# The down projection of the last two token blocks by two levels of seven products, in an attention and SwiGLU kernel

## The chip, the cores and the metric

One core of a Trainium2 chip runs the kernel; the other cores are idle. The metric is the time of one execution on the device in microseconds. The profile is that of one execution, taken by the hardware profiler; its times count from the first instruction of the program.

## The reference

Everything is float32. The attention has no softmax: for each of 8 batches and 8 heads `kv = k^T v` (64 x 64) and `out = q kv`, then an RMS norm over the 64 features of the head with a gain. The heads side by side give 4608 token rows of 512 features. The feed-forward part is

```python
g = x @ w_gate                          # 4608 x 512 by 512 x 1536
silu = g * (1.0 / (1.0 + np.exp(-g)))
val = x @ w_val                         # 512 x 1536
return silu * val @ w_out               # 1536 x 512
```

## The kernel before

The tokens are cut into 9 blocks of 512 (`NB` = 9). Each block has an attention part (`Att`), an up phase (gate and value products, then `silu(g) * val`, whose result `h` stands with the 1536 features on partitions) and a down phase (`h` times `w_out`). Blocks 0, 1, 2 run alone; from block 3 on (`PAIRED`) two blocks go through the up phase together (`Pair.up`), and then down one after the other (`Ffn.down` for `pair.a`, then for `pair.b`). The last pair is blocks 7 and 8, and no attention work lies beside it.

The matrix products use the Winograd form of Strassen's scheme: both operands are cut in 2 x 2 quadrants and seven products of sums take the place of eight. Product numbers 1 to 7 name them; `CHAIN` says in which of three PSUM accumulators (`a`, `b`, `c`) each product lands and whether it starts it. Products 1, 6, 7, 4 follow each other in one bank of `b`, and 5, 3 in one of `c`. Between two products of one bank the sum so far is copied or added out to SBUF, so the next product has to wait for that eviction. The pools hold three banks of `b`, two of `c`, one of `a` and two of `m` (scratch).

In a pair's up phase two levels of the scheme are nested: 7 outer times 7 inner products. It runs in 6 units (`j`), each with 4 groups of outer products (`Inner.GROUPS` = (1, 5), (6, 2), (7), (4, 3)), each group with 7 inner products. A group of two outers issues two 128x256 matmuls per product, a group of one issues one. Group 0 evicts mostly by ScalarE copies, all other evictions are VectorE additions. The last two products of a group (3 and 4) are issued inside the sequence of the next group. `made1`, `made2` and `made3` hold what follows: GpSimd adds partial results, ScalarE applies Silu, GpSimd multiplies the two halves into `h` (for the last unit VectorE does), and `h_sums` forms the side sums that the down phase of block a needs, again on GpSimd. The weights of the up phase, 49 leaf sums per unit, were written to DRAM once and are streamed through nine `t` tiles (`Stream`): a load goes out when the tile nine loads back is free.

The down phase before is one level: 7 products per block, each 6 steps (`NP`) times 2 output halves of 128x256, so 84 matmuls per block, with `h` as the stationary operand and `w_out` or a sum of its quadrants as the moving one. GpSimd forms these sums (`turn_t`) and the side sums of block b (`second_sums`). With no further block the last pair uses the branches marked `lone`, and block 8 also those marked `final`: product 3 goes into its own banks of `m`, is split in two halves, and each half is added and stored on its own, so that the end is short.

The order of instructions on an engine comes from a list scheduler that works in the program's trace order and takes what it thinks is ready. `in_order(engine)` pins an engine to trace order; before, it holds for TensorE in the down phases of pairs. `tc.issue_after(ins)` queues the instructions traced inside it behind `ins`, on the engine of `ins` alone; it makes nothing wait for `ins` to finish. In a queue each engine works in order: an instruction that waits holds all behind it.

Lines that matter: 661 the matmuls of `Quad`, 816 those of `Inner`, 1032 those of `third`; 130, 131 and 132 the helpers `add`, `sub` and `mul` (most vector work has one of these lines, whatever it is for); 494 and 510 transposes of the attention part on TensorE and VectorE; 1122 the output stores.

Of the kernel before, what the change touches and what calls it, by code (L numbers as in the profile page):

```python
# [18 lines left out]
def kernel(  # L19
# [620 lines left out]
    class Quad:  # L640


        def __init__(self, steps):
            self.steps = steps
            self.ps, self.room = {}, None

            self.apart = {}

# [3 lines left out]
        def multiply(self, p):  # L652
            name, first = CHAIN[p]
            if first:
                tiles = [PSUMS[name].tile([P, 2, HB], F32, name=name) for _ in range(1 + (name in self.apart))]
                self.ps[name], self.apart[name] = tiles[0], tiles[-1]
            banks = self.ps[name], self.apart[name]
            for e, i in self.order(p):
                lhsT, rhs = self.operands(p, e, i)

                self.ffn.multiplied = nc.tensor.matmul(  # L661
                    banks[e][:, e], lhsT=lhsT, rhs=rhs, start=first and i == 0 and (e == 0 or banks[0] is not banks[1]),
                    stop=i == self.steps - 1, skip_group_check=True,
                )
# [92 lines left out]
    class Inner:  # L757
# [94 lines left out]
        def made3(self, p, e, q):  # L852
# [7 lines left out]
            mul(engine, h[:, :, :, 0:HB], halves(c11), halves(c12))  # L860
            with tc.issue_after(self.ffn.fifth.ins):
                nc.scalar.activation(out=c21, in_=c21, func=ACT.Silu)
            mul(engine, h[:, :, :, HB:BLK], halves(c21), halves(c22))
            self.ffn.ended = self.ffn.a.h_sums(self.j, 1, engine)

# [13 lines left out]
    class Stream:  # L879
# [15 lines left out]
        def pump(self):  # L895

            while self.next and not self.held[-9]:
                n, j, c = key = self.next.pop(0)
                tile_ = t_tile(key)
                os, ps = JOINT[c]  # L900
# [6 lines left out]

        def use(self, n, j, o, p):
            c, i = self.joint[o, p]
            key = n, j, c  # L910
# [74 lines left out]
    class Down(Quad):  # L985
        def __init__(self, ffn):
# [3 lines left out]
            self.final = ffn.n == NB - 1  # L990
            self.lone = False
            self.opens = None
            self.keeps = False
            if self.final:
                self.apart["c"] = None
# [16 lines left out]
        def multiply(self, p, es=(0, 1)):  # L1012
            if p == 3 and self.lone:
                self.third(es)
                return
# [7 lines left out]
        def third(self, es):  # L1023


            if es[0] == 0:
                tiles = [m_psum.tile([P, 2, HB], F32, name="m") for _ in range(1 + self.final)]
                self.thirds = tiles[0], tiles[-1]
            for e in es:
                for i in range(self.steps):  # L1030
                    lhsT, rhs = self.operands(3, e, i)
                    self.ffn.multiplied = nc.tensor.matmul(  # L1032
                        self.thirds[e][:, e], lhsT=lhsT, rhs=rhs, start=i == 0 and (e == 0 or self.final),
                        stop=i == self.steps - 1, skip_group_check=True,
                    )
            if not self.final:
                add(nc.vector, self.o1[:, :, HD:DM], self.thirds[0], self.u2)
                self.ffn.store(self.o1, 0)
                return
            for e in es:  # L1040
                add(nc.vector, self.o1[:, e, HD:DM], self.thirds[e][:, e], self.u2[:, e])
                self.ffn.store(self.o1[:, e : e + 1, HD:DM], e, slice(HD, DM))

        def after6(self):
            super().after6()
            if self.lone:
                self.add_c(self.u2, self.u2)

        def order(self, p):
            order = [(e, i) for e in range(2) for i in range(self.steps)]  # L1050
            return order if p == 3 and self.final else sorted(order, key=lambda ei: ei[1])
# [17 lines left out]
        def rows(self):  # L1069
            o = ring()  # L1070
            self.o1, self.o2 = o[:, 0:2], o[:, 2:4]

        def after2(self):
            if self.lone:
                self.rows()
            add(nc.vector, self.o1[:, :, 0:HD], self.ps["a"], self.s)
            if self.final:
# [398 lines left out]
```

## Time and profile before

| | us |
|---|---|
| median of 3 runs | 1013.04 (1010.67 to 1013.1) |
| the profiled execution | 1012.7 |
| its span, first to last instruction | 1010.9 |
| TensorE busy | 993.7 |
| VectorE busy | 673.7 |
| GpSimd busy | 369.6 |
| last up phase, blocks 7 and 8 | 807.6 to 934.9 |
| last down phases, blocks 7 and 8, TensorE | 934.9 to 1007.5 |
| from there to the end of the span | 3.4 |

The profile has one row for each group of like instructions: start, how long they took together, engine, line, operation, output <- inputs, shape, count. A number in brackets at the end is idle time of the engine before it and who ended it. `PE` is TensorE, `DVE` VectorE, `ACT` ScalarE, `POOL` GpSimd, `SPq` SyncE's DMA queue. A float32 matmul leaves two records, so a count of 24 means 12 matmuls. In a table of windows the columns are the window's length, then busy time and number of instructions of PE, PEld (weight loads), DVE, ACT and POOL, the granted TensorE clock, the busy share of the DMA engines and GB/s.

### The profile page before, as it was taken

What the parts mean: (1) busy time and instruction counts of PE and PEld (TensorE: products, weight loads), DVE (VectorE), ACT (ScalarE), POOL (GpSimd) and SP (SyncE); (2) the same over time, 40 slices, a digit from 0 to 9 for tenths busy, and PEclk for the clock granted to TensorE, in tenths of its full rate; (3) what the DMA queues carried; (4) which work ended last, traced back from release to release, by engine and by line L of the source; (5) the groups of instructions that cost most, each with busy time, mean ns of one, the idle gap of its engine ahead of it and who ended that gap; (6) DMA issues with size and microseconds to landing.
All of it is one profiled execution on the core that took longest, in us unless ns stands there. A gap on an engine that the chain in (4) does not pass through costs nothing.

```text
span 1010.9 us, 17078 instructions
## 1 busy us (share of the span) xinstructions
PE 993.7 (98%) x6506; PEld 831.6 (82%) x6506; DVE 673.7 (67%) x1121; ACT 232.2 (23%) x367; POOL 369.6 (37%) x290
## 2 busy tenths in 40 slices
PE   5999999999999999999999999999999999999998
PEld 4544688888888888888888888888888888888887
DVE  2999797589868477656676746666668566666311
ACT  2665111221122311212211121121112121121000
POOL 0000263255544240445456004455660026546600
PEclk9999999999999999999999999999999999999999
DMA  8688653483866855767742464667221654553011
GB/s 220 198 266 260 120 93 136 97 288 97 210 136 122 214 114 158 189 179 182 170 130 42 111 164 135 182 164 191 77 42 43 146 164 144 150 145 101 1 42 42
DMA packets 254290, 143.23 MB, mean 142 GB/s; under 512 B 149504, under 2 KB 236544, under 8 KB 254208
## 3 DMA queue, kind: packets, MB, share of 16 engines
q1 hardware_dynamic: 223488, 138.20, 50.8%
q10 hardware_dynamic: 30656, 3.94, 2.5%
q8 instruction: 52, 0.85, 0.4%
q14 instruction: 30, 0.25, 0.1%
q0 software_dynamic: 64, 0.00, 0.0%
HBM read 104.99 MB, written 28.70 MB: 132 GB/s over the span
## 4 chain that ended last, share of the span: by engine, by line
PE 75%; DMA 1%; POOL 0%; SPq 0%; issue 0%; DVE 0%; POOLq 0%
PE b L816 22%; PE b L661 20%; PE c L816 11%; PE c L661 9%; PE a L816 5%; PE a L661 5%; PE m L431 1%; PE m L1032 1%; PE m L370 1%; DMA ld<-in_v_dram 1%; POOL t L131 0%; SPq L312 0%; PE b L370 0%; PE b L431 0%; PE a L431 0%
## 5 line engine op out<-in xcount | busy, mean ns | idle before, releaser
L816 PE MATMUL b<-arena,t 128*128 128x256 f32 x1008 | 244.5, 381 | 0.0
L816 PEld LDWEIGHTS b<-arena,t 128*128 128x128 f32 x1008 | 190.1, 190 | 29.6 <-DVE r L130 2.4
L130 POOL TENSOR_TENSOR r<-r 128x256 f32<-128x256 f32 (+1 forms) x90 | 94.7, 1054 | 246.1 <-DVE r L130 154.9
L130 DVE TENSOR_TENSOR r<-b,r 128x512 f32<-128x512 f32 (+1 forms) x234 | 138.9, 606 | 60.1 <-PE b L816 54.8
L130 DVE TENSOR_TENSOR r<-c,r 128x512 f32<-128x512 f32 (+1 forms) x170 | 104.5, 623 | 81.9 <-PE c L816 40.1
L132 POOL TENSOR_TENSOR arena<-r 128x1024 f32<-128x1024 f32 (+1 forms) x54 | 102.1, 1904 | 112.3 <-DVE r L130 67.9
L131 POOL TENSOR_TENSOR t<-wo 128x512 f32<-128x512 f32 x54 | 76.9, 1445 | 167.8 <-DVE wo L130 105.9
L130 DVE TENSOR_TENSOR r<-a,r 128x512 f32<-128x512 f32 x93 | 59.2, 636 | 108.3 <-PE a L661 70.7
L816 PE MATMUL c<-arena,t 128*128 128x256 f32 x504 | 122.5, 379 | 0.0
L131 DVE TENSOR_TENSOR arena<-arena 128x512 f32<-128x512 f32 (+3 forms) x96 | 104.3, 1101 | 20.0 <-PE b L661 17.7
L816 PEld LDWEIGHTS c<-arena,t 128*128 128x128 f32 x504 | 95.6, 190 | 13.5 <-issue 0.3
L661 PE MATMUL b<-wo,arena 128*128 128x256 f32 x432 | 98.1, 382 | 0.2
L661 PE MATMUL b<-t,arena 128*128 128x256 f32 x432 | 96.2, 379 | 0.0
L661 PEld LDWEIGHTS b<-wo,arena 128*128 128x128 f32 x432 | 81.2, 190 | 12.5 <-DVE arena L132 0.9
L661 PEld LDWEIGHTS b<-t,arena 128*128 128x128 f32 x432 | 82.1, 190 | 11.2
L830 ACT COPY r<-b 128x512 f32<-128x512 f32 x54 | 31.7, 586 | 189.9 <-PE b L816 189.9
L131 POOL TENSOR_TENSOR t<-arena 128x512 f32<-128x512 f32 x36 | 51.1, 1432 | 56.2 <-PE c L661 21.9
L816 PE MATMUL a<-arena,t 128*128 128x256 f32 x252 | 66.1, 379 | 0.0
L816 PEld LDWEIGHTS a<-arena,t 128*128 128x128 f32 x252 | 47.9, 190 | 6.5
L661 PE MATMUL c<-t,s 128*128 128x256 f32 x216 | 48.1, 379 | 0.0
L661 PE MATMUL a<-wo,arena 128*128 128x256 f32 x216 | 48.1, 379 | 0.0
L661 PEld LDWEIGHTS a<-wo,arena 128*128 128x128 f32 x216 | 41.0, 190 | 5.6
(115 smaller groups left out, 1242.9 us busy)
## 6 DMA issues: line engine op xcount, KB each, us to landing
t<-w SPq DMA_DIRECT2D x180, 256.0 KB, 3.1
out_dram<-r SPq DMA_DIRECT2D x17, 512.0 KB, 2.9
ld<-in_k_dram SPq DMA_DIRECT2D x26, 288.0 KB, 4.6
ld<-in_v_dram SPq DMA_DIRECT2D x26, 288.0 KB, 6.1
t<-w SPq DMA_DIRECT2D x54, 128.0 KB, 2.3
ld<-in_moe_w_gate_dram SPq DMA_DIRECT2D x12, 512.0 KB, 4.6
ld<-in_moe_w_val_dram SPq DMA_DIRECT2D x12, 512.0 KB, 4.7
ld<-in_moe_w_out_dram SPq DMA_DIRECT2D x12, 512.0 KB, 4.8
```

The source lines that it names most:

```text
L130: add = lambda e, o, a, b: e.tensor_tensor(out=o, in0=a, in1=b, op=OP.add)
L131: sub = lambda e, o, a, b: e.tensor_tensor(out=o, in0=a, in1=b, op=OP.subtract)
L132: mul = lambda e, o, a, b: e.tensor_tensor(out=o, in0=a, in1=b, op=OP.mult)
L370: self.positions = nc.tensor.matmul(self.kv_ps[r][u * D : (u + 1) * D, g, :], lhsT=k[:, u, c, :], rhs=v[:, u, c, :], start=(c == 0), stop= ...
L431: self.multiplied = nc.tensor.matmul(self.ps[i][u][p : p + D, t, j, :], lhsT=self.qt[rows, tile_t, head, p : p + D], rhs=kvs[b % 3][rows, ...
L661: self.ffn.multiplied = nc.tensor.matmul(banks[e][:, e], lhsT=lhsT, rhs=rhs, start=first and i == 0 and (e == 0 or banks[0] is not banks[1 ...
L816: self.ffn.multiplied = nc.tensor.matmul(ps[:, i], lhsT=stream.use(self.ffn.n, self.j, o, p), rhs=self.operand(o, p), start=first and i == ...
L830: copied = nc.scalar.copy(out=dst, in_=ps)
L1032: self.ffn.multiplied = nc.tensor.matmul(self.thirds[e][:, e], lhsT=lhsT, rhs=rhs, start=i == 0 and (e == 0 or self.final), stop=i == self ...
```

## The change

For the last pair a new class `Deep` takes over the down phase of both blocks at once. It cuts `w_out` and `h` twice: 7 outer times 7 inner products, each of 3 steps of 128x128 weights against 256 columns (128 tokens of each block). Now the weight is the stationary operand and `h` the moving one, so the output comes out transposed, features on partitions. `Last` is the group class for it; its order of products and sums is written out by hand in `Deep.down`, inside `in_order` for TensorE and VectorE.

The sums of weight quadrants that this needs are formed on VectorE during the last up phase: `prepare` lists 6 turns of `w_out` in place, 12 sums that are kept, and 9 leaf groups (three sums and a DMA write to DRAM each); `tick`, called after each product of that phase, takes a step from the list at every second call, inside `tc.issue_after` of the product just traced. `made` replaces the last part of `made3`: the second multiplication, then the side sums of `h` for both blocks at once, and after every second unit the two sums of `turn` (the inner level's sums on `h`), put on `due` for 16 calls later. The 21 leaf weights come back through `Stream` in the `t` tiles. The sums on `h` of the inner level (`sum_x`) and of the outer level (`outer`) are made on VectorE inside the down phase.

At the end two of the four output corners are transposed on VectorE in 32x32 blocks and stored in 16 DMAs each, in runs of 32 floats (`send`; one corner through ScalarE's queue, one through SyncE's). The other two are transposed on TensorE, copied out by ScalarE, the last by VectorE, and stored in 8 DMAs (`turn_back`).

The branches `lone`, `final`, `third`, `apart` and `rows` go from `Quad`, `Down` and `Ffn`; blocks before the last pair never took them.

```diff
@@ class Inner, made3
             mul(engine, h[:, :, :, 0:HB], halves(c11), halves(c12))
+            if self.ffn.deep:
+                self.ffn.deep.made(self.j, engine, c21, halves(c21), halves(c22), h)
+                return
             with tc.issue_after(self.ffn.fifth.ins):
                 nc.scalar.activation(out=c21, in_=c21, func=ACT.Silu)
             mul(engine, h[:, :, :, HB:BLK], halves(c21), halves(c22))
             self.ffn.ended = self.ffn.a.h_sums(self.j, 1, engine)
+
+    class Last(Inner):
+        GROUPS = ((1, 2), (6, 5), (7,), (4, 3))
...
+        def multiply(self, p, cs=(0, 1, 2)):
...
+            for c in cs:
+                for i, o in enumerate(self.outers):
+                    self.ffn.multiplied = nc.tensor.matmul(
+                        ps[:, i], lhsT=self.deep.weight(o, p, c), rhs=self.deep.operand(o, p, c),
+                        start=first and c == 0 and i == 0, stop=c == 2, skip_group_check=True,
+                    )
...
+    class Deep:
+        LEAVES = (5, 7, 4)
...
+        def prepare(self, temp):
...
+            for i, o in enumerate(self.LEAVES):
+                b = self.quadrant({5: 3, 7: 1, 4: 2}[o])
+                for c in range(3):
+                    rows = slice(2 * c, 2 * c + 2)
+                    raw = temp[:, 0:4].rearrange("p (k n) d -> p k (n d)", k=2)
+                    self.later += [
+                        lambda b=b, rows=rows, raw=raw: sub(nc.vector, raw, b[:, rows], self.quadrant(6)[:, rows]),
+                        lambda: sub(nc.vector, temp[:, 4], temp[:, 0], temp[:, 1]),
+                        lambda: sub(
+                            nc.vector, temp[:, 5:7], temp[:, 2:4], temp[:, 1:2].to_broadcast([P, 2, P])
+                        ),
+                        lambda i=i, c=c: nc.sync.dma_start(out=self.dram[:, i, c], in_=temp[:, 0:7]),
+                        None, None,
+                    ]
+
+        def tick(self):
+            self.count += 1
+            if self.count % 2:
+                return
+            steps = self.later
+            if self.due and self.due[0][0] <= self.count:
+                steps = [self.due.pop(0)[1]]
+            step = steps.pop(0) if steps else None
+            if step:
+                with tc.issue_after(self.pair.multiplied.ins):
+                    step()
+
+        def made(self, j, engine, c21, g, v, h):
+            def second():
+                mul(engine, h[:, :, :, HB:BLK], g, v)
+                a11, a21, a22 = h[:, :, 0, 0:HB], h[:, :, 0, HB:BLK], h[:, :, 1, HB:BLK]
+                add(engine, a21, a21, a22)
+                sub(engine, a21, a21, a11)
+
+            with tc.issue_after(self.pair.fifth.ins):
+                nc.scalar.activation(out=c21, in_=c21, func=ACT.Silu)
+            if j == NP - 1:
+                self.second = second
+                return
+            second()
+            if j % 2:
+                self.due += [(self.count + 16, step) for step in self.turn(j // 2, (0, 1))]
...
+            return [lambda: add(nc.vector, a21, a21, a22), lambda: sub(nc.vector, a21, a21, a11)]
...
+        def send(self, room, half, cols, queue):
...
+                        queue.dma_start(
+                            out=dst.rearrange("(c i) j -> i c j", i=32), in_=t[32 * r : 32 * (r + 1), f, e]
+                        )
...
+        def down(self):
+            g = [Last(self, i) for i in range(4)]
...
+            m(0, 7)
+            self.outer(5, ((0, 0), (0, 1)))
+            m(0, 3)
+            m(1, 1)
...
+            m(2, 4)
+            nc.vector.transpose(out=room[:, 0], in_=c11)
+            self.send(room[:, 0], 0, 0, nc.scalar)
+            m(3, 6)
+            add(nc.vector, c22, u3, c22)
+            m(3, 5)
+            nc.vector.transpose(out=room[:, 1], in_=c22)
+            self.send(room[:, 1], 1, 1, nc.sync)
+            m(3, 2)
+            m(3, 7)
+            self.rows = ring().rearrange("p (e q) (o f d) -> p e q o f d", e=2, o=2, f=2)
+            m(3, 3)
+            self.turn_back(0, 0)
+            self.turn_back(1, 1)
+            m(3, 4)
+            self.turn_back(1, 0)
+            self.turn_back(0, 1, True)
@@ class Pair
-            a.down_ = Down(a)
-            a.down_.keeps = True
-            a.down_.turn_t(5)
+            if not deep:
+                a.down_ = Down(a)
+                a.down_.keeps = True
+                a.down_.turn_t(5)
@@ the loop over pairs
+        if pair.deep:
+            stream.leaves(pair.deep)
+            pair.up(fill)
+            with in_order(nc.tensor.engine, nc.vector.engine):
+                pair.deep.down()
+            continue
         pair.up(fill)
```

## The prediction

> **What bounds the kernel now.** I read the page's busy shares and its chain, then the windows over the last 200 us, then the timelines of one unit of the last up phase, and last a place where VectorE and GpSimd both work on SBUF.
>
> ```profile
> PE 993.7 (98%) x6506; PEld 831.6 (82%) x6506; DVE 673.7 (67%) x1121; ACT 232.2 (23%) x367; POOL 369.6 (37%) x290
> 811.00:935.00 124.00, 124.00 (x575) 108.87 (x574) 84.27 (x143) 24.00 (x33) 65.79 (x53) 1.00 0.47 139
> 935.00:1008.00 73.00, 72.54 (x337) 63.52 (x335) 16.77 (x20) 5.75 (x9) 16.29 (x12) 1.00 0.08 28
> ...
> 934.85 5.34 PE L661 MATMUL b<-wo,arena 128*128 128x256 f32 x24
> 1004.78 2.75 PE L1032 MATMUL m<-wo,arena 128*128 128x256 f32 x12
> 1007.58 0.42 DVE L130 TENSOR_TENSOR r<-m,r 128x256 f32<-128x256 f32 x1 [7.35 <-PE m L1032]
> ...
> 898.61 0.69 DVE L130 TENSOR_TENSOR r<-c,r 128x512 f32<-128x512 f32 x1
> 899.47 0.69 DVE L130 TENSOR_TENSOR r<-c,r 128x512 f32<-128x512 f32 x1 [0.17 <-PE c L816]
> 900.33 0.69 DVE L130 TENSOR_TENSOR r<-b,r 128x512 f32<-128x512 f32 x1 [0.17 <-PE b L816]
> 901.86 1.46 PE L816 MATMUL b<-arena,t 128*128 128x256 f32 x6
> 896.04 4.68 POOL L132 TENSOR_TENSOR arena<-r 128x1024 f32<-128x1024 f32 x2 [3.79 <-DVE r L130]
> 900.80 0.73 POOL L130 TENSOR_TENSOR s<-arena 128x256 f32<-128x256 f32 x1
> 901.60 0.73 POOL L131 TENSOR_TENSOR arena<-s,arena 128x256 f32<-128x256 f32 x1
> ...
> 138.61 3.16 DVE L131 TENSOR_TENSOR arena<-arena 128x512 f32<-128x512 f32 x2
> 138.25 9.40 POOL L131 TENSOR_TENSOR t<-arena 128x512 f32<-128x512 f32 x6 [1.33 <-DVE arena L130]
> ```
>
> TensorE is the bound and has no gap in the last up phase (124.00 of 124) or in the last down phase (72.54 of 73), so a product left out is worth its whole time, and a product that starts late costs its whole delay. A down product is 24 records from 934.85 to the next at 940.03, 0.216 us each; one 128x256 matmul is two records, 0.432 us. In the up phase VectorE is 68% busy and empties PSUM just behind TensorE, a 0.69 us eviction in each 0.86 us product, so its queue has little slack. The third block is unit j = 4 of that phase: evictions of (group 1, product 5), (group 0, product 3) and (group 1, product 6); the last must be out before group 1's product 7 reuses the bank at 901.86. Beside them GpSimd multiplies (896.04) and forms the side sums of the unit before (900.80, 901.60).
>
> **What the Trainium skill says.** "GPSIMD Engine Reference", section 1 (Specifications), says that GpSimd's SBUF interfaces are shared with VectorE, with contention where a VectorE instruction has two SBUF inputs. The trace agrees strongly: from 138.61 on a 128x512 sum with both inputs in SBUF takes 1.58 us beside GpSimd, against 0.68 alone (800.31); each waits out the GpSimd instruction in hand. PSUM evictions have one SBUF input and stay at 0.69 beside GpSimd. "DMA: Bandwidth & Descriptors", Specifications, says that runs below 512 B make the DMA engine read, modify and write; no row of before stores such runs to HBM, so the trace is silent on that.
>
> **Down phase: what goes and what comes.** Before, two blocks x 7 products x 12 matmuls = 168; 72.5 us. After, 7 x 7 x 3 = 147 matmuls of the same form: 147 x 0.432 = 63.5, so 9.1 us go. Sixteen transposes come; the eight of the first attention block took 1.06 us less a 0.16 us tail, 0.113 each: +1.8. Between the last product and the last four transposes stands one 0.69 us eviction, of which 0.45 lies under the four transposes before it: +0.4. TensorE's down phase: 65.7, that is -6.8.
>
> VectorE gets 72 instructions there: 33 of 768 elements, 19 of 512, 13 of 256, 7 of 1024. By the pitch that rows of before show (0.60 for 512, 1.67 for 1536, 1.09 ns an element and 0.05), 53 us in 66. I laid them in their queue's order beside the products. Sums for product 5 of the first group end 5 us after the start and are wanted at 7.8; the nearest comes at the second group's product 1, whose sum ends about 14.7 and is wanted at 16.0. GpSimd is idle by then, so nothing is held. No stall: 0, and if every sum were a third slower, +3. The 21 leaf loads (192 KB, 2.8 us in before) run nine tiles ahead of TensorE on a DMA at 8%: nothing.
>
> The end: two corners leave by VectorE transposes and 16 stores each of 128 B runs (32 KB), one set from ScalarE's queue, one from SyncE's. The nearest rows are loads of 32 KB in such runs (2.3 us) and SBUF copies of 64 KB (3.5 us); I take 2.5. Four at a time per queue, SyncE's set starts 55 us into the phase and is issued at about 64; eight stores of 0.5 us follow, the last at 68.2, landed at 70.8. From TensorE's end that is 4.9 us, where before had 3.35 (1007.53 to 1010.88): +1.5. Down phase in all: -6.8 + 1.5 = **-5.3**. With stores of 5 us it would be +8.5 later.
>
> GpSimd loses the nine t<-wo sums and the second block's sums, which nothing waits for in time; free of charge. The dropped special cases for the last block only ran here.
>
> **Up phase: what is added.** 49 side sums on VectorE: 15 of 512 elements, 12 of 384, 9 each of 256 and 128, 4 of 1024; 23.9 us at the pitch above, in 39.7 idle us. Their amount fits; their places matter. The source hangs them behind a TensorE product, but that wrapper orders only instructions of the named instruction's own engine, and these are VectorE's: in the built program's order they stand where the scheduler found VectorE free. The first four sums on wo stand even before the phase's first eviction; there the inner sums end about 1 us later and meet about 1.7 us of slack: 0.
>
> (a) The turn of h rows. For units 0 and 1 its two 1024-element sums stand in unit 2, just before and behind the eviction (group 1, product 6); for units 2 and 3 in unit 4, before and behind (group 0, product 3). They wait for GpSimd's sums of the unit just finished. These now cover both blocks, 512 elements, 1.27 us each (the t<-wo row) instead of 0.73: done at 900.80 + 2.54 = 903.35 on the ruler above. Unit 2: sum 903.45 to 904.6, eviction to 905.2, wanted at 901.86: 3.3 us. Unit 4: sum to 904.6, eviction of product 3 to 905.2, second sum to 906.4, eviction of product 6 to 907.1: 5.2 late, less about 1.5 us of group 2 products that the new order puts ahead: 3.7. Together 7.0. From below 0 cannot be reached, as VectorE's queue is in order (2.5 each if GpSimd is a little quicker); above, 5.2 each.
>
> (b) The other sums hold VectorE when GpSimd has the interface. The 512-element sum of a leaf often follows (group 1, product 1), about 898.5, when the second 2.35 us multiplication has just begun: up to 2.2 us; the small ones after it wait out a 1.27 us sum. In unit 3: 900.75 + four rows of 0.6, 0.6, 0.3 and 0.69 plus 0.2 held gives 903.1 against 901.86, about 1.3 to 1.5. In unit 1 two such places, 0.6 and 0.7; in unit 3 another 0.5 before group 2's product 7; 0.1 elsewhere. Sum 3.5, bounds 0 and 5; other places find GpSimd idle. Each later product moves by these: nothing downstream wins them back.
>
> Sum: 7.0 + 3.5 - 5.3 = **+5.2** against the profiled execution of 1012.7 (1.8 around its span): 1017.9, rounded to 1018.0. The median shown is 1013.04, 0.3 above that execution, well inside this.
>
> **Rivals.** *B: the shared interface costs nothing in the new place*, only the in-order wait (a): 7.0 - 5.3 = +1.7, 1014.4. For it: only some of the leaf sums fall on a multiplication. Against: the rows from 138 on.
>
> *C, faster: the sums find their gaps.* If GpSimd's chain ends before VectorE gets to the turn, or TensorE's order gives other work to fill, the up phase loses 0 to 2 and the down phase's gain stands: 1007.5 to 1009.5, taken 1008. For it: 39.7 idle us for 23.9 of sums. Against: the eviction's deadline is 1.5 us, GpSimd's chain 7.3 us.
>
> *D, slower still: 128 B stores to HBM.* At 5 us each the queues drain at 1.25 us a store, ScalarE's copies of the turned tiles wait behind its 16, then SyncE's eight come last: 8.5 us more, 1026.5. It decides from about 3 us a store. For it: the skill's sentence. Against: 128 B reads land in 2.3.
>
> *E: leaf writes hold VectorE.* Its scratch tile is rewritten only when the write has landed (2.6 us for the nearest w<-r rows, some 3 us of room): up to +1 each in three places, near 1021.
>
> **How the numbers follow.** Forecast A 0.50 (own range 1015 to 1022), B 0.17, C 0.15, D 0.12, E 0.06. Likeliest: 1018.0. The range 1008 to 1026 leaves out half of C and half of D and less than that of the rest. A change below 0.3% (3 us) is what a measurement of this kernel can't tell from none; slower by more: most of A, D, E and a third of B, 0.67; within: most of B, a little of A and C, 0.17; faster: 0.16.
>
> **What would show it.** Right: TensorE gaps of some 3 us each in units 2 and 4 of the last up phase, released by a VectorE eviction behind a 1024-element sum that waits for GpSimd; shorter ones in units 1 and 3; the down phase about 66 us on TensorE with no gap but the 0.4 before the last transposes; 4 to 5 us from there to the end. Wrong: an up phase of 127 us as before (C); 128x512 sums at 0.68 beside GpSimd's multiplications (B); landing of the small stores above 3 us and ScalarE's turned copies late (D).

## The result, and the profile after

The changed kernel takes **1024.12 us** (median of 4 runs, 1023.04 to 1024.53), the kernel before 1012.34 beside it: ratio **1.0117, 95% interval 1.0099 to 1.0134**. It is slower, by 11.8 us; the forecast was 1018.0. The profiled execution has a span of 1022.3 us (before 1010.9).

In the kernel after, line 813 has the matmuls of `Inner` (816 before), 889 those of the new down phase, 1073 its transposes on TensorE, 1064 and 1083 the stores, 962 the leaf writes. First the busy shares on the page of after, then its windows over the last up phase and the last down phase:

```profile
PE 992.8 (97%) x6480; PEld 828.0 (81%) x6480; DVE 736.6 (72%) x1223; ACT 232.9 (23%) x370; POOL 357.6 (35%) x275
...
811.00:951.66 140.66, 130.46 (x575) 111.93 (x574) 106.73 (x188) 24.25 (x33) 70.11 (x50) 0.95 0.54 165
951.66:1018.00 66.34, 65.64 (x311) 57.34 (x309) 54.55 (x72) 6.55 (x12) 0.00 (x0) 1.00 0.27 64
```

The up phase is where the time is lost. TensorE runs the same 575 records there as before but is busy for 130.46 of 140.66 us, and the last column but two, the granted clock, is 0.95. From the first `Inner` matmul to the first matmul of the down phase it lasts 143.80 us (807.86 to 951.66), before 127.26: **+16.5**. From there to the end it is 70.64 us, before 76.03: **-5.4**. The timeline of the end, with TensorE's last row and VectorE's behind it, then the small stores from ScalarE's and SyncE's queues:

```profile
1017.11 0.63 PE L1073 MATMUL m<-ident,r 128*128 128x128 f32 x4 [0.44 <-DVE r L130]
1017.78 0.76 DVE L1077 COPY r<-m 128x256 f32<-128x256 f32 x2 [0.81 <-PE m L1073]
...
1002.77 7.95 ACTq L1064 DMA_DIRECT2D out_dram<-r  x16
...
1006.91 7.83 SPq L1064 DMA_DIRECT2D out_dram<-r  x16
```

TensorE ends at 1017.74, the span 4.6 later. The only gap of TensorE in the down phase is the 0.44 in the first line. Sixteen small stores take 7.9 us of a queue, 0.5 each, and land in 1.7 us (ScalarE's) and 1.9 us (SyncE's), medians.

By unit, the up phase loses 1.3 us in unit 1, 6.8 in unit 2, 1.3 in unit 3, 7.1 in unit 4 and nothing in 0 and 5. The timeline of unit 2, by engine (GpSimd, VectorE, TensorE):

```profile
856.09 5.14 POOL L132 TENSOR_TENSOR arena<-r 128x1024 f32<-128x1024 f32 x2 [4.43 <-DVE r L130]
...
862.65 1.26 POOL L131 TENSOR_TENSOR arena<-arena 128x512 f32<-128x512 f32 x1
...
858.94 1.27 DVE L130 TENSOR_TENSOR r<-c,r 128x512 f32<-128x512 f32 x2
863.95 1.23 DVE L130 TENSOR_TENSOR arena<-arena 128x1024 f32<-128x1024 f32 x1 [3.74 <-POOL arena L131]
865.09 0.68 DVE L130 TENSOR_TENSOR r<-b,r 128x512 f32<-128x512 f32 x1
...
861.14 0.59 PE L813 MATMUL b<-arena,t 128*128 128x256 f32 x2
865.83 2.07 PE L813 MATMUL b<-arena,t 128*128 128x256 f32 x4 [4.10 <-DVE r L130]
867.70 2.77 PE L813 MATMUL c<-arena,t 128*128 128x256 f32 x6
```

Read it from the bottom. TensorE stops at 861.73 and waits 4.10 us for the eviction at 865.09. VectorE has that eviction next in its queue, but the turn's 1024-element sum stands ahead of it and waits 3.74 us for GpSimd's sum, which ends at 863.91. That is the wait the prediction described. The last row is what it did not describe: six records take 2.77 us where six took 1.46 before. The windows of two microseconds show why (the third number from the end is the granted clock):

```profile
862.00:864.00 2.00, 0.00 (x0) 0.00 (x0) 0.05 (x1) 0.00 (x0) 1.84 (x2) 0.98 0.43 144
864.00:866.00 2.00, 0.17 (x1) 0.17 (x2) 2.00 (x3) 0.00 (x0) 0.00 (x0) 0.50 0.00 0
870.00:872.00 2.00, 2.00 (x9) 1.68 (x8) 1.31 (x3) 0.00 (x0) 0.73 (x1) 0.82 0.16 47
```

TensorE's clock falls to half at about 863.9, in the middle of the gap, and stays there until 870.7: 6.8 us. Unit 4 is alike: a gap of 4.00, then 6.8 us at half clock. Units 1 and 3 have one gap of 1.05 us each and keep their clock. In unit 3 a small sum stands ahead of the eviction beside GpSimd's second multiplication (the timelines of VectorE, GpSimd and TensorE):

```profile
888.38 1.24 DVE L131 TENSOR_TENSOR s<-s 128x128 f32<-128x128 f32 x1
889.54 0.68 DVE L130 TENSOR_TENSOR r<-b,r 128x512 f32<-128x512 f32 x1
...
884.34 5.13 POOL L132 TENSOR_TENSOR arena<-r 128x1024 f32<-128x1024 f32 x2 [4.89 <-DVE r L130]
...
890.28 1.56 PE L813 MATMUL b<-arena,t 128*128 128x256 f32 x6 [1.05 <-DVE r L130]
```

A 128x128 sum takes 0.28 us when nothing holds it (871.11); here it ends at 889.6, just after GpSimd's pair of multiplications (889.47).

So the ledger of the up phase is: turn waits 4.10 + 4.00 = 8.1; records at half clock about 2.5 + 3.0 = 5.5 (the longer rows of the two stretches against the same rows of before; it is less than half of 6.8 each, as 1.9 and 1.0 us of the two stretches still lie in the gaps); units 1 and 3, 2.6; and 0.3 that the two long gaps leave out, since each is counted from the end of the row before it (861.14, two records in 0.59 us) and not from where the next record was due (0.43). Sum 16.5.

### The profile page after: what moved, and what is told of

It reads as the page before. It is cut to its first block, busy times and chain, and to the rows that moved or that the text cites. A ratio compares the mean times of both kernels' runs of the same rounds, so it can differ in the third digit from the quotient of the medians.

```text
span 1022.3 us, 17217 instructions
## 1 busy us (share of the span) xinstructions
PE 992.8 (97%) x6480; PEld 828.0 (81%) x6480; DVE 736.6 (72%) x1223; ACT 232.9 (23%) x370; POOL 357.6 (35%) x275
## 4 chain that ended last, share of the span: by engine, by line
PE 70%; DMA 2%; DVE 2%; POOL 1%; issue 1%; DVEq 0%; SPq 0%; POOLq 0%
PE b L813 20%; PE b L658 16%; PE c L813 10%; PE c L658 8%; PE a L813 5%; PE a L658 4%; PE b L889 4%; PE c L889 2%; DMA leaf<-s 1%; DVE r L130 1%; PE m L431 1%; PE a L889 1%; PE m L370 1%; POOL arena L132 1%; DMA ld<-in_v_dram 1%
## 5 line engine op out<-in xcount | busy, mean ns | idle before, releaser
L813 PE MATMUL b<-arena,t 128*128 128x256 f32 x1008 | 248.0, 384 | 6.2 <-DVE r L130 6.2
L813 PEld LDWEIGHTS b<-arena,t 128*128 128x128 f32 x1008 | 191.4, 192 | 38.2 <-DVE r L130 10.2
L130 DVE TENSOR_TENSOR r<-b,r 128x512 f32<-128x512 f32 (+1 forms) x247 | 145.2, 601 | 58.7 <-PE b L813 47.3
L131 DVE TENSOR_TENSOR arena<-arena 128x512 f32<-128x512 f32 (+5 forms) x119 | 121.7, 1040 | 9.2 <-PE b L658 6.9
L131 POOL TENSOR_TENSOR t<-wo 128x512 f32<-128x512 f32 x45 | 64.2, 1447 | 163.7 <-DVE wo L130 106.2
L658 PE MATMUL b<-wo,arena 128*128 128x256 f32 x336 | 76.8, 382 | 0.2
L658 PE MATMUL b<-t,arena 128*128 128x256 f32 x336 | 74.8, 379 | 0.0
L658 PEld LDWEIGHTS b<-wo,arena 128*128 128x128 f32 x336 | 62.9, 190 | 10.1 <-DVE arena L132 0.9
L658 PEld LDWEIGHTS b<-t,arena 128*128 128x128 f32 x336 | 63.8, 190 | 8.7
L813 PE MATMUL a<-arena,t 128*128 128x256 f32 x252 | 66.1, 379 | 0.0
L130 DVE TENSOR_TENSOR arena<-arena 128x512 f32<-128x512 f32 (+4 forms) x46 | 39.9, 883 | 9.3 <-POOL arena L131 8.9
L658 PE MATMUL b<-arena 128*128 128x256 f32 x192 | 45.5, 380 | 0.0
L658 PE MATMUL b<-arena,t 128*128 128x256 f32 x192 | 45.4, 379 | 0.0
```

What stands on the lines that cost most here:

```text
L130: add = lambda e, o, a, b: e.tensor_tensor(out=o, in0=a, in1=b, op=OP.add)
L131: sub = lambda e, o, a, b: e.tensor_tensor(out=o, in0=a, in1=b, op=OP.subtract)
L658: self.ffn.multiplied = nc.tensor.matmul(ps[:, e], lhsT=lhsT, rhs=rhs, start=first and i == 0 and e == 0, stop=i == self.steps - 1, skip_g ...
L813: self.ffn.multiplied = nc.tensor.matmul(ps[:, i], lhsT=stream.use(self.ffn.n, self.j, o, p), rhs=self.operand(o, p), start=first and i == ...
```

## The experiments

Each run's up phase and the rest of its span, taken as above from its profile, and its time. The kernel before measured 1011.6 to 1012.1 beside them.

| run | up phase | to the end | time, us | ratio to before, 95% |
|---|---|---|---|---|
| before | 127.3 | 76.0 | 1012.3 | |
| after | 143.8 | 70.6 | 1024.1 | 1.0117 (1.0099 to 1.0134) |
| e1 | 136.7 | 70.2 | 1015.6 | 1.0033 (1.0016 to 1.0050) |
| e2 | 137.1 | 70.2 | 1018.2 | 1.0055 (1.0035 to 1.0075) |
| e3 | 130.0 | 76.0 | 1014.1 | one run |
| e4 | 144.6 | 71.0 | 1026.1 | 1.0135 (1.0116 to 1.0155) |
| e5 | 132.8 | 71.1 | 1013.1 | 1.0007 (1.0000 to 1.0015) |
| e7 | 153.9 | 71.0 | 1034.5 | 1.0225 (1.0210 to 1.0240) |
| e8 | 153.6 | 76.0 | 1038.6 | one run |
| e9 | 130.7 | 70.2 | 1011.2 | 0.9992 (0.9983 to 1.0000) |
| e10 | 137.2 | 70.2 | 1018.3 | 1.0060 (1.0045 to 1.0074) |
| e11 | 130.6 | 70.5 | 1010.2 | 0.9982 (0.9976 to 0.9989) |
| e12 | 133.9 | 70.5 | 1014.3 | 1.0023 (1.0015 to 1.0031) |

The third column settles the down phase: all nine other runs with the new one have 70.2 to 71.1 us there, whatever their up phase does. The rest is about the up phase. (e6 has no row: it was to be e1 with a second scratch tile for the leaf sums, and the tile does not fit in SBUF.)

### One half alone: e9 and e10

```diff
 # e9
-            if j % 2:
-                self.due += [(self.count + 16, step) for step in self.turn(j // 2, (0, 1))]
 # e10, prepare: zeros in the kept and scratch tiles, of each leaf only the write
+            for t in self.kept.values():
+                nc.vector.memset(t, 0.0)
...
-                        lambda b=b, rows=rows, raw=raw: sub(nc.vector, raw, b[:, rows], self.quadrant(6)[:, rows]),
...
```

> The kernel after, with the turn's four sums of the first four units (units 2 and 4) left out, so that the down phase multiplies hidden values that were not turned. What stays is the leaf part alone. Theory (turn: gaps of 8.1 us and 5.5 us of halved clock; leaf: two gaps of 1.05 us and small holds): time about 1024.1 - 8.1 - 5.5 = 1010.5, between 1009 and 1013. Rival (as in the run with the gap filled, leaf writes and holds come to light as soon as the turn's long gaps don't cover them): 1013 to 1018.

> The kernel after, with the leaf sums, the kept sums and the sums of the down weights left out (zeros in their tiles, leaf writes and loads as before). What stays is the turn alone. Theory: both gaps of 4 us in units 2 and 4 stay, with their 6.8 us of halved clock each, the gaps of units 1 and 3 go: time 1024.1 less 2 to 4 us, 1020 to 1022.5. Rival (the turn waits are only as long because VectorE is crowded with leaf sums): gaps under 3 us and the clock held, 1010 to 1014.

Without the turn the time is 1011.2 (expected 1009 to 1013), 12.9 below after. Without the leaf sums it is 1018.3, 5.8 below, more than expected: the turn's gaps are still there, but of 2.86 and 2.87 us instead of 4.10 and 4.00, and the half clock lasts 3.4 us after each instead of 6.8 (TensorE's row of unit 2, then the window before the half clock and the window of it):

```profile
863.16 2.08 PE L813 MATMUL c<-arena,t 128*128 128x256 f32 x4 [2.86 <-DVE r L130]
...
859.42:862.83 3.41, 0.88 (x5) 0.42 (x3) 1.55 (x2) 0.20 (x1) 1.75 (x2) 1.00 0.50 160
862.83:866.25 3.42, 3.09 (x7) 2.35 (x8) 3.03 (x5) 0.00 (x0) 0.73 (x1) 0.50 0.00 0
```

For e9 the theory holds. In e10 neither side does: the gaps are under 3 us as its rival had it, but the clock isn't held. Alone, the turn adds 10.0 us to the up phase and the leaf sums add 3.5; together 16.5. The 3.0 over come from the turn's gaps. A gap can be read as the length of GpSimd's chain (its multiplications and the two sums behind them), less the time that TensorE still has products to run from the chain's start, plus 1.9 for the sum and the eviction: 7.35 - 6.40 + 1.9 in both units of e10; 7.82 - 5.64 + 1.9 and 7.35 - 5.27 + 1.9 in after. TensorE stops after the same 30 records in both kernels. What the leaf sums change is that the chain starts later beside these records, by 0.8 us in unit 2 and 1.1 in unit 4, and that the multiplications of unit 2 take 5.14 us instead of 4.67. The rows of VectorE and GpSimd in unit 4 of after show the later start:

```profile
904.29 0.69 DVE L131 TENSOR_TENSOR s<-wo 128x512 f32<-128x512 f32 x1 [3.09 <-DMA leaf<-s]
906.63 0.68 DVE L130 TENSOR_TENSOR r<-a,r 128x512 f32<-128x512 f32 x1
...
906.86 4.67 POOL L132 TENSOR_TENSOR arena<-r 128x1024 f32<-128x1024 f32 x2 [4.80 <-DVE r L130]
```

A leaf sum waits 3.09 us until the last leaf write has left its scratch tile; the evictions behind it are late, and GpSimd's multiplication waits for them. Unit 2 has the same wait, of 2.71 us. No gap of TensorE stands right behind these two waits, but they make the turn's gaps longer, and with 1.2 and 1.1 us more the half clock lasted twice as long.

### What a gap costs: e3 and e8

```diff
+                if self.ffn.n == NB - 2 and self.g == 1 and p == 6 and self.j in DELAYS:
+                    with tc.issue_after(self.ffn.evicted.ins):
+                        behind = nc.vector.tensor_reduce(out=delayed[:, self.j : self.j + 1],
+                            in_=arena[:, 0 : DELAYS[self.j]], axis=mybir.AxisListType.X, op=OP.add)
...
-                    add(nc.vector, dst, ps, self.onto(e, q))
+                    with tc.issue_after(behind.ins) if behind else ExitStack():
+                        self.ffn.evicted = add(nc.vector, dst, ps, self.onto(e, q))
```

> The kernel before with four useless VectorE reductions of 2000, 3000, 4000 and 5000 elements a partition, in units 1, 2, 3 and 4 of the last up phase, ahead of one eviction each, to make TensorE wait for graded times (an estimate: 1.2, 2.3, 3.3 and 4.3 us). It measures the price of a gap by itself, without turn, leaf or down phase. Theory (a gap of some 4 us takes the clock down to 0.50 for some 6 us, one of 1 us doesn't): the unit with the longest gap is longer by the gap and by 2.5 to 3 us more, the unit with the shortest by the gap alone; which of the two middle gaps sets it off tells where the step is. Rival (the halved clock has to do with the turn's own work, power on VectorE and GpSimd together): the clock stays at 1.00 after all four gaps, and each unit is longer by its gap alone.

> The kernel before with the reductions of e3 made longer: 6500, 7000, 7500 and 9000 elements in units 1 to 4. In e3 a reduction of 4.31 us made a gap of 0.43 us and one of 5.35 us a gap of 1.47 us, so these should make gaps of about 3.0, 3.5, 4.1 and 5.7 us. Theory: a gap of over some 3.4 us takes the clock to 0.50, for 5 to 7 us, and the unit is longer by the gap and 2.5 to 3.5 us more; e1's 2.54 us gap did not. So at least the gaps of units 3 and 4 do it. Rival (the turn's own work is what lowers the clock): clock 1.00 after all four, each unit longer by its gap alone.

Both are the kernel before with a useless reduction on VectorE. In e3 only two made TensorE wait: the estimate of the gaps had missed that an eviction has slack. Reductions of 4.31 and 5.35 us made gaps of 0.43 and 1.47. In e8, VectorE's first and last reduction and TensorE's rows behind all four:

```profile
836.21 6.92 DVE L832 TENSOR_REDUCE delayed<-arena 128x1 f32<-128x6500 f32 x1
917.00 9.52 DVE L832 TENSOR_REDUCE delayed<-arena 128x1 f32<-128x9000 f32 x1
...
843.77 1.55 PE L818 MATMUL b<-arena,t 128*128 128x256 f32 x4 [3.03 <-DVE r L132]
870.43 1.13 PE L818 MATMUL b<-arena,t 128*128 128x256 f32 x4 [3.55 <-DVE r L132]
898.11 1.27 PE L818 MATMUL b<-arena,t 128*128 128x256 f32 x4 [4.07 <-DVE r L132]
927.17 4.93 PE L818 MATMUL b<-arena,t 128*128 128x256 f32 x10 [5.64 <-DVE r L132]
```

In all six the gap is the hold less 3.88 us: that is this eviction's slack, in the order that the scheduler gives TensorE in these two runs. All four gaps of e8 brought the half clock, for 3.4, 3.4, 3.4 and 6.8 us; that of 3.03 us too, where the theory asked for more than 3.4. The gaps of e3, and one of 2.54 us in e1, did not. The up phase grew by 26.3 us, of which all gaps are 16.9; the 9.4 left are near half of the 17 us at half clock, 8.5. What is lost behind each gap comes to 1.8, 2.3, 2.1 and 3.2. No turn or leaf sum is in this kernel, so the rival falls: **the gap alone lowers the clock, and this adds 1.8 to 3.2 us to its length.**

The length of a gap does not settle it alone. In every profile the clock changes only at instants that lie whole multiples of 3.413 us apart: the two half-clock stretches of after start 51.20 us apart (15 times that), those of e8 27.31 us each (8 times). Here are windows cut at these instants: before and in e8's first stretch, the same for unit 2 of after, and around e1's gap of 2.54 us (883.12 to 885.66). The number after the window's length is how long TensorE was busy, the third from the end the clock:

```profile
840.94:844.36 3.42, 0.58 (x3) 0.53 (x4) 3.42 (x4) 0.00 (x0) 0.00 (x0) 1.00 0.13 37
844.36:847.77 3.41, 3.41 (x10) 2.67 (x9) 2.83 (x6) 0.00 (x0) 2.14 (x3) 0.50 0.02 5
...
860.50:863.91 3.41, 1.23 (x6) 0.75 (x4) 0.00 (x0) 0.56 (x1) 3.25 (x3) 1.00 0.64 193
863.91:867.32 3.41, 1.49 (x4) 1.22 (x5) 3.37 (x4) 0.00 (x0) 0.01 (x1) 0.50 0.00 0
867.32:870.74 3.42, 3.42 (x10) 2.70 (x9) 1.78 (x5) 0.00 (x0) 1.45 (x2) 0.50 0.00 0
...
880.32:883.73 3.41, 2.80 (x13) 2.11 (x12) 3.41 (x3) 0.43 (x1) 3.41 (x2) 1.00 0.40 125
883.73:887.14 3.41, 1.48 (x7) 1.33 (x8) 3.41 (x6) 0.00 (x0) 3.25 (x3) 1.00 0.07 20
```

The clock of a window follows how busy TensorE was in the window before it. Ahead of all ten stretches inside the programs (after, e7, e8, e10) TensorE was busy for 1.23 us or less of the 3.41; in none of the 13 profiles did a window at full clock with 1.48 us or more bring the half clock. A stretch went on after a window with 2.73 us or less and ended after one with 3.09 or more. So it matters how a gap falls on the windows: e1's 2.54 us lie 0.61 in one and 1.93 in the next and cost nothing more, while of the 2.86 us in e10 2.54 lie in one. No run was made to move a gap across the windows; this is read from the profiles on record.

"TensorE: Matmul & The Clock Gate", Part 1 of the Trainium skill, "What's actually happening", describes this: a gate that halves TensorE's clock after an idle window of about 3.4 us and opens after a busy one, with windows that run freely. The steps of 3.413 us agree. That 3.4 us of idle are needed does not: the gap of 2.86 us in e10 was enough, and a window in which TensorE still worked for 1.23 us (after).

### Filling the gap: e4

```diff
+            if self.ffn.deep and self.g == 1 and p == 7 and self.j in (2, 4):
+                idle = m_psum.tile([P, 2, 2, P], F32, name="m")
+                with tc.issue_after(self.ffn.multiplied.ins):
+                    for k in range(8):
+                        behind = nc.tensor.matmul(idle[:, 0], lhsT=ident, rhs=x_both[:, :, 0, 0, 0:P], start=True, stop=True)
```

> The kernel after with eight useless 128x256 matmuls, whose product is never read, in the two gaps of units 2 and 4, so that TensorE is busy for about 2 of the 4 us. The wait itself stays. Theory (the clock falls because TensorE idles for long): the two stretches at clock 0.50 go and 4 to 6 us with them, time 1018 to 1020.5. Rival (the slow records after the gaps have another cause, such as the sums on VectorE or the SBUF reads of the turn): no gain, 1023 to 1026.

The matmuls filled 3.6 us, more than the 2 meant. The clock stayed at 1.00 in all windows of both places, and the time did not fall: 1026.1, where even the rival said 1023 to 1026. TensorE's rows of unit 2, and a VectorE row between them:

```profile
860.13 3.62 PE L817 MATMUL m<-arena,ident 128*128 128x256 f32 x16
865.40 1.56 PE L822 MATMUL b<-arena,t 128*128 128x256 f32 x6 [1.66 <-DVE r L130]
869.16 1.56 PE L822 MATMUL b<-arena,t 128*128 128x256 f32 x6 [0.89 <-DVE r L130]
872.90 1.56 PE L822 MATMUL b<-arena,t 128*128 128x256 f32 x6 [1.75 <-DVE r L130]
...
871.02 0.69 DVE L131 TENSOR_TENSOR s<-wo 128x512 f32<-128x512 f32 x1 [1.59 <-DMA leaf<-s]
```

In unit 4, where no leaf sum is left, the stretch with the gap became shorter by 1.8 us (16.97, after 18.79), though filler and rest of the gap are 5.2 us there (913.15 to 918.36) against 4.0: the half clock's 3 us went. In unit 2 the stretch became 1.8 longer (20.21, after 18.43): TensorE at full clock now came early enough to wait twice more for VectorE, once behind a held small sum, once behind a leaf sum that waited 1.59 us for its scratch tile. In after, at half clock, no gap stands at either place. So the 5.5 us of the ledger are what happened, not what is won by keeping the clock.

### The order on VectorE: e1 and e2

```diff
 # e1, Inner.multiply
-                add(nc.vector, dst, ps, dst)
+                self.ffn.evicted = add(nc.vector, dst, ps, dst)
...
 # e1, tick
-            steps = self.later
+            steps, behind = self.later, self.pair.multiplied
...
-                steps = [self.due.pop(0)[1]]
+                steps, behind = [self.due.pop(0)[1]], self.pair.evicted
...
-                with tc.issue_after(self.pair.multiplied.ins):
+                with tc.issue_after(behind.ins):
 # e2, on e1
-            steps, behind = self.later, self.pair.multiplied
+            steps, behind = self.later, self.pair.evicted or self.pair.multiplied
```

> The kernel after with one edit: the side sums of the turn (two rows in units 2 and 4) are queued behind VectorE's last eviction at the time they come due, so that no eviction stands behind them. Leaf sums as in the kernel after. Theory (the turn sums make VectorE wait for GpSimd's multiplications, TensorE idles some 4 us in units 2 and 4 and then has half its clock for some 6 us): both 4 us gaps and both stretches at clock 0.50 go, time about 1024.1 - 8.4 - 5.5 = 1010.2 us, between 1009 and 1013. Rival (VectorE simply has too much to do in these units, wherever the sums stand): the gaps move to another place and the time stays at 1020 or more. Second rival (the turn is late at its other end: the next pair of operands or the down phase waits for the sums): the time falls by less than 6 us and a new gap stands at a later matmul.

> As the run before, and the leaf sums, the kept sums and the sums of the down weights are queued behind VectorE's last eviction too. Theory (the 1.05 us gaps in units 1 and 3 come from side sums that stand ahead of an eviction while GpSimd holds the shared port): these gaps shrink, and the time is about 2 us under the run before, near 1008. Rival (the gaps of units 1 and 3 come from the amount of work on the port, not from the order): the time is that of the run before within 1 us.

Tied to an eviction, an instruction of the same engine, the turn does stand where the source has it: in unit 2 its sums start at 869.07 and 871.58, after GpSimd's last (865.65). Both long gaps and both stretches of half clock went, as the theory says, and 8.5 us with them; but 1015.6 is short of 1010.2. Gaps of 6.3 us in all stand elsewhere now. VectorE's rows of two leaf sums, GpSimd's row beside the second, and TensorE's:

```profile
855.20 0.69 DVE L131 TENSOR_TENSOR s<-wo 128x512 f32<-128x512 f32 x1 [5.04 <-DMA leaf<-s]
879.95 2.71 DVE L131 TENSOR_TENSOR s<-wo 128x512 f32<-128x512 f32 x1 [0.34 <-DMA leaf<-s]
...
879.75 5.11 POOL L132 TENSOR_TENSOR arena<-r 128x1024 f32<-128x1024 f32 x2 [3.21 <-DVE r L130]
...
885.66 1.99 PE L813 MATMUL b<-arena,t 128*128 128x256 f32 x8 [2.54 <-DVE r L130]
```

The second sum starts beside the first multiplication and ends after it, 2.71 us later instead of 0.69; the small sum behind it takes 1.23 beside the second. In e2, with the leaf sums tied too, eleven gaps of 0.2 to 1.0 us stand in units 1 to 5, 6.1 us in all; the up phase is as long as e1's and the time 2.6 us longer: the theory for e2 falls. Tied to the last eviction, leaf sums still come beside GpSimd's multiplications (2.26, 2.27 and 2.00 us for one sum each in units 2, 3 and 4). The order alone does not do it. Nor are waits for leaf writes needed for such gaps: no VectorE row of e2's up phase waits for one (in e1 one does for 5.04 us).

### Clear of GpSimd: e5, and everything on GpSimd: e7

```diff
 # e5, on e2
         def tick(self, g, k):
             self.count += 1
-            if self.count % 2:
+            if g == 1 or (g == 0 and k > 2):
                 return
 # e7, on e1: in prepare
-                            nc.vector, self.kept[o][:, x], b[:, :, k, n], b[:, :, 0, 1]
+                            nc.gpsimd, self.kept[o][:, x], b[:, :, k, n], b[:, :, 0, 1]
```

(In e5 one more empty step follows each leaf. In e7 all sums of `prepare` move.)

> All side sums are queued behind VectorE's last eviction, and come due only in groups 2 and 3 and at the first three products of group 0, when GpSimd has no long multiplication of the unit to do. Theory (what is left of the loss in e1 and e2, gaps of 6.1 to 6.3 us, comes from side sums that wait for GpSimd's hold of the shared port while evictions stand behind them, and from the leaf writes): gaps of TensorE in the up phase fall to 2 us or less, time 1007 to 1010, faster than before. Rival (VectorE's amount of work a unit is the bound, wherever it is put): gaps stay at 5 us or more, moved into groups 2 and 3, time 1014 to 1018.

> As e1, with the leaf sums, the kept sums and the sums of the down weights on GpSimd instead of VectorE. Theory (evictions read one operand from PSUM and one from SBUF and are not held, two operands from SBUF are): no eviction stands behind a side sum that waits for the port, TensorE's gaps fall below 3 us as long as GpSimd keeps up: time 1008 to 1013. Rival (GpSimd, which has 10 to 11 of 21 us a unit to do already, becomes late with its multiplications, and ScalarE and the ring of tiles behind it): new gaps in TensorE with VectorE waiting for GpSimd, time 1015 or more.

In e5 the gaps shown fell to 2.45 us, a little over the 2 expected, and the up phase by 4.3 against e2, and GpSimd's pair of multiplications in unit 2 takes 4.68 us again (5.12 in e2): the clash with GpSimd is a cause. But the phase is 5.5 us longer than before, so about 3 us are in waits too short for the view, and the time ties with before, 1013.1, outside the 1007 to 1010 expected.

In e7 the rival came true by a way it did not name. GpSimd's, SyncE's and TensorE's rows:

```profile
818.48 11.52 POOL L131 TENSOR_TENSOR ld<-wo 128x384 f32<-128x384 f32 x12
...
832.46 0.33 SPq L962 DMA_DIRECT2D leaf<-s  x1
832.88 2.23 SPq L1208 DMA_DIRECT2D t<-w  x4
...
835.78 2.90 PE L813 MATMUL c<-arena,t 128*128 128x256 f32 x6 [10.92 <-DMA t<-w]
```

The scheduler put GpSimd's side sums in one row, from 805 to 832. The second leaf write waits for the last of them in SyncE's queue, and the weight loads stand behind that write: none is issued from 816.0 to 832.9, and TensorE idles for 10.92 us.

### The turn on GpSimd: e11, and spread sums: e12

```diff
 # e11, on e5: made1, behind the last small sum of group 1
+            added = add(nc.gpsimd, self.shared[2][:, 1, :, e, q], u2[:, :, e, q], r5[:, :, e, q])
             if p == 4:
+                while self.ffn.deep and self.ffn.deep.due:
+                    with tc.issue_after(added.ins):
+                        added = self.ffn.deep.due.pop(0)()
 # tick
-            if g == 1 or (g == 0 and k > 2):
+            if g == 1 or (g == 0 and k > 2) or (g == 3 and j in (2, 4) and k < 6):
 # e12, on e11: prepare, in each leaf
-                        None, None, None,
+                        kept.pop(0) if kept else None, kept.pop(0) if kept else None, None, None, None,
```

(The turn's sums, which wait in `due`, take GpSimd as their engine.)

> The run with all sums clear of GpSimd's multiplications, changed in one thing: the turn's four sums run on GpSimd itself, right behind its last small sum of group 1, and no leaf sum comes due beside them. Theory (what is left there, 5.5 us of up phase with 2.5 us in gaps that the trace shows and the rest in waits too short to be shown, is VectorE's amount of work in the sums' units; the turn is 9 to 10 us of that): the up phase falls to 128.5 to 131 us and the time to 1008 to 1011, faster than before by 0.1 to 0.4 per cent. Rival (GpSimd's next long sum and multiplication come late behind the turn and ScalarE and VectorE wait for them; or the sums of VectorE stand against GpSimd's hold again): time 1012 or more.

> The run with the turn on GpSimd, with the twelve kept sums no longer in one row in units 0 and 1 but two at a time in the idle steps of the first six leaf pieces. In that run the up phase was still 3.3 us longer than before, and the only gaps of TensorE that the trace shows, 0.55 and 0.42 us, stand in units 0 and 1, where VectorE was busy for 19.7 of 20 us. Theory (a crowd of side sums makes evictions late by small waits): the two gaps go, the up phase falls to 128 to 129.5 us and the time by 1 to 2.5 us, to 1008 to 1009.5. Rival (the 3.3 us are spread over all units and come from single sums beside GpSimd's hold): no change within 0.7 us of 1010.2.

e11 is **faster than both kernels: 1010.2 us, ratio 0.9982 (0.9976 to 0.9989)**. On GpSimd the turn stands behind the sums that it needs in the same queue, so nothing on VectorE waits for the chain. GpSimd's rows of the turn in unit 2, and the window over the up phase:

```profile
866.21 2.36 POOL L130 TENSOR_TENSOR arena<-arena 128x1024 f32<-128x1024 f32 x1
868.65 2.36 POOL L131 TENSOR_TENSOR arena<-arena 128x1024 f32<-128x1024 f32 x1
...
808.00:936.00 128.00, 126.96 (x578) 108.10 (x577) 103.20 (x185) 24.43 (x33) 80.08 (x54) 1.00 0.60 182
```

The up phase is 3.3 us longer than before, with gaps of 0.55 and 0.42, both in unit 1 (98 records are a unit). e12 was to remove these and failed, 1014.3: the new list brought leaf sums beside the turn in units 2 and 4. One row each of GpSimd, VectorE and TensorE:

```profile
867.46 2.80 POOL L130 TENSOR_TENSOR arena<-arena 128x1024 f32<-128x1024 f32 x1
...
868.31 2.10 DVE L131 TENSOR_TENSOR s<-s 128x128 f32<-128x128 f32 x1
...
871.06 1.13 PE L813 MATMUL b<-arena,t 128*128 128x256 f32 x4 [1.64 <-DVE r L130]
```

One 128x128 sum, 0.28 us by itself, takes 2.10 beside GpSimd and costs TensorE 1.64. e12 changed both places at once, but its profile tells them apart. The first matmul of unit 2 starts 42.46 us after the phase's first in before, 45.15 in e11 and 44.38 in e12. So 2.7 of e11's 3.3 us lie in units 0 and 1, where the kept sums stand; spreading them won 0.8 there, and the units after lost 4.1, of which 1.64 and 1.83 are two gaps behind leaf sums beside the turn.

## Why the prediction was wrong

**The step that failed** is the pricing of a late product: "a product that starts late costs its whole delay". In after each long gap costs that and then 2.5 and 3.0 us more, as TensorE comes back at half clock. This term, 5.5 us of the +16.5, stood at nothing in the prediction. e8 shows it with none of the change in it, and in e4 the clock stays up when TensorE is kept busy in the gap. The kernel before has no gap long enough in the stages read, so no row of those stages could have shown it; the page of the Trainium skill that could was not used.

**(a) The turn**: mechanism, place and releaser right; 4.10 and 4.00 us where 3.3 and 3.7 were written, 8.1 for 7.0. That it came so near is in part luck. The term took GpSimd's chain as it stands in before; with the turn alone (e10) the gaps are 2.86 and 2.87. The leaf sums add the rest, by the later start of the chain (0.8 and 1.1) and, in unit 2, by 0.46 as GpSimd's pair of multiplications takes 5.14 us, not 4.68; the leaf sums hold GpSimd as it holds them.

**(b) The shared interface**: 2.6 for 3.5 (the terms written for it add to 3.2 to 3.4), in units 1 and 3 as said, one place each.

Without the clock, (a) and (b) with the 0.3 beside the gaps make 11.0 for the 10.5 forecast, one too high and one too low, and the time would have been near 1018.6. That is arithmetic; e4 shows that keeping the clock does not bring it.

**Down phase**: -5.4 for -5.3. TensorE 66.1 us for 65.7, tail 4.6 for 4.9, no stall by VectorE.

**Rivals.** B (nothing for the interface): wrong, by the rows of units 3 (after) and 2 (e12). C (the sums find their gaps): not in this order; e11, with the turn moved, comes nearest: 3.3 us of up phase for C's 0 to 2, 1010.2 for its 1008. D (slow stores): 0.5 us each instead of 1.25, landed in 1.7 and 1.9 instead of 5, wrong. E (leaf writes hold VectorE): right in part. VectorE waits 10.2 us for them in after; no gap of TensorE stands right behind, but in units 2 and 4 these waits go with the later start of the turn's chain, 0.8 and 1.1 us, and in e4 a wait of 1.59 has a gap right behind it.

## What to carry to other kernels

Price a gap of TensorE in two parts, its length and what the clock takes after it. Here the second part was nothing where no window of 3.41 us had more than 1.93 us of idle in it, about 2 us where the clock came back after one window, and 2.5 to 3.2 after two. A gap of 2 to 4 us can therefore go either way, by where it falls (an estimate from these windows). An engine's idle time holds side work only where its inputs are ready and its port is free: four sums that wait for GpSimd did most of the harm here, and on GpSimd itself they cost little. To place an instruction, tie it to one of its own engine, and look past the engine at the queues behind it, SyncE's among them.

## What was not expected of the hardware

The half clock comes in steps of 3.41 us at fixed instants, and hangs on how busy TensorE was in the window just ended, not on the length of the gap alone. Two gaps of about 4 us differ by it: 4.00 in unit 4 of after reached 1.02 us into the next window and cost two steps, 4.07 in e8 cost one.

That a VectorE sum waits out the GpSimd instruction beside it was in the prediction (1.58 us for a 128x512 sum); here a 128x128 sum of 0.28 us took up to 2.10, a 128x512 one 2.71. That the hold goes the other way too was not: two multiplications of GpSimd took 5.14 us in place of 4.68 with such sums beside them.
